# Where the sums of a fast matrix product, their casts and their low parts stand in the order of a kernel written out by hand

## The chip, the cores and the metric

The kernel runs on one core of a Trainium2 chip. The metric is the device time of one execution in microseconds (us). Engines: TensorE (PE) multiplies, VectorE (DVE), ScalarE (ACT) and GpSimd (POOL) work element by element, SyncE (SP) issues the DMAs. Each engine runs its own instructions strictly in the order in which they were emitted.

## The reference, cut to what matters

```python
# q, k, v: (2 batches, 8 heads, 768 tokens, 64) f32; lam: one decay per head
out = decay_attention(q, k, v, lam)           # in blocks, with a decaying state
x = out.transpose(0, 2, 1, 3).reshape(1536, 512)
h = x @ w_in;  x = (h * tanh(softplus(h))) @ w_out      # 512 -> 2048 -> 512, mish
h = x @ w_in2; return (h * sigmoid(h)) @ w_out2         # the same sizes, silu
```

All is f32. The weights reach the chip as 64-bit floats and are decoded there.

## The kernel before

Attention comes first: 12 chunks of 128 tokens, each giving 128 columns of x. Then two layers, mm 0 and mm 1, over three token tiles of 512 (t = 0, 1, 2). A weight block n (0 to 15 in layer 0, 16 to 31 in layer 1) has an input half (n, 0) and an output half (n, 1), of 128x512 each. `emit_h(t, n)` makes one 128x512 tile of the hidden values with 12 matmuls, `emit_o(t, n)` adds its share to four output banks with 12 more.

**Precision.** Each f32 operand is split into a high part (a cast on ACT to fp32r: xh, wh, gh, sh, th) and a low part (value minus high part: xl, wl, gl, sl, tl), and three of the four cross products are multiplied. The low parts of weights (`run_parts`, L175 and L176) and of hidden values (`activate`, L395 to L399) are made on POOL.

**Decoding.** `split_w(n, i)` queues five DVE operations (L129 to L137) in `todo`; from the middle of group 4 on the first of them runs on ACT (L93). The fifth frees one of the four load slots, and `pump` then issues the next load on SP. `run_split(k)` emits the next k operations of `todo`. A finished decode goes to `parts`; the next `run_parts` emits its cast and low part. `dec` has four buffers.

**Steps and groups.** Twelve steps (the loop at L621) interleave attention with layer 0 for the first blocks. Step 8 is the first without attention. From step 8 on the kernel also prepares a fast product for tiles 0 and 1: with x cut in quarters, seven products (`Block.m1` to `m7`, six matmuls each, L535) stand for eight. Four of their x operands are `sums[0]` to `sums[3]`, made once per layer from the quarters: f1 = a21 + a22 (sum 0), f2 = f1 - a11 (sum 1), f3 = a11 - a21 (sum 2), a12 - f2 (sum 3). The weights get four subtractions too, `sum_pair(p)` (L161), through a one-buffer tile `t4` that f3 of layer 0 and s1 of layer 1 share.

Seven groups g = 1 to 7 follow, of four weight blocks each (n0 = 4g), two blocks A and B of seven products each. A group is a list of 30 items, emitted in order (L686): the products, four fills (the outputs of tile 2 from the group before), o(0,f) and o(1,f) (outputs of tiles 0 and 1), and hs (hidden values of tile 2). After each item come the parts, `run_rest`, `run_sums` and `run_split`. In groups 1 and 4 (`g in (1, NG)`, the first of each layer) the order of the A products leaves room: A.m1, fill, A.m2, fill, fill, A.m5, A.m6, fill, A.m7, A.m3, A.m4.

Within a block A.m1 is copied by ACT to bank b (L554) before A.m2 continues in its bank; A.m5 is copied by ACT (L559); after m6 DVE adds b to that into c (L543), after m7 into e; m7 waits for the first add and m4 for the second.

**Sums before.** `make_sums` (layer 0) queues fourteen single operations in `summing`, where `xsplit` is a cast on ACT with its low part on DVE; steps 8 to 11 each emit four. `evac` of tile 1 at the end of group 3 queues seven entries for layer 1; there two of the four low parts run on POOL. Each of the next items emits two entries (`run_sums(2)`). The tiles' own casts and low parts are `part(j)` (L465, L467): the cast at once, the low part on POOL from the queue `rest`, one for each item, without regard to the tile.

Of the kernel before, what the change touches and what calls it, by code (L numbers as in the profile page):

```python
# [17 lines left out]
def decay_attention_mish_silu_kernel(  # L18
# [353 lines left out]
    def bank(name):  # L372
        nbank[0] += 1
        if late and nbank[0] % 2:
            return late[2].tile([P, T], F32, tag="x", name=name)
        return ps_h.tile([P, T], F32, tag="h", name=name)

    def run_rest(k):
        for _ in range(min(k, len(rest))):
            rest.pop(0)()  # L380

    def run_sums(k):
        for _ in range(min(k, len(summing))):
            summing.pop(0)()

    def run_later():
        while later:
# [15 lines left out]
    def emit_h(t, n, first=False):  # L403
        mm = n // NF
        xt = x_tile(t)
        assert (n, 0) in ready
# [12 lines left out]
        activate(ph, mm, t, n)  # L419
# [20 lines left out]
        if last:  # L440
            evac(mm, n % NF // GF, t)

    def xsplit(hi, lo, f, eng=None):
        nc.scalar.copy(hi, f)
        (eng or nc.gpsimd).tensor_tensor(out=lo, in0=f, in1=hi.bitcast(F32), op=ALU.subtract)

    def evac(mm, g, t):
        if g == 0:
            accs[mm, t] = (accp if t == 0 else late[1]).tile([P, 4, T], F32, tag="acc", name="acc")
        acc = accs[mm, t]  # L450
        for j in range(4):
# [12 lines left out]
        def part(j):  # L464
            nc.scalar.copy(xh[:, j, :], acc[:, j, :])  # L465
            rest.append(
                lambda: nc.gpsimd.tensor_tensor(  # L467
                    out=xl[:, j, :], in0=acc[:, j, :], in1=xh[:, j, :].bitcast(F32), op=ALU.subtract
                )
            )  # L470
# [6 lines left out]
        s1 = late[0].tile([P, 2, T], F32, tag="t4", name="s1", bufs=1)  # L477
        tt, add, sub = nc.vector.tensor_tensor, ALU.add, ALU.subtract

        s2, s3, s4 = a1[:, 0:2], a2[:, 0:2], a1[:, 2:4]  # L480
        summing.extend([
            lambda: tt(out=s1, in0=a2[:, 0:2], in1=a2[:, 2:4], op=add),
            lambda: xsplit(*sums[0], s1, nc.vector),
            lambda: (tt(out=s3, in0=a1[:, 0:2], in1=s3, op=sub), tt(out=s2, in0=s1, in1=s2, op=sub)),  # L484
            lambda: (xsplit(*sums[1], s2), tt(out=s4, in0=s4, in1=s2, op=sub)),
            lambda: xsplit(*sums[2], s3, nc.vector),
            lambda: xsplit(*sums[3], s4),
            lambda: (part(2), part(3)),
        ])

    sums = []
# [2 lines left out]
    def make_sums():  # L494

        x0, x1 = x_tile(0), x_tile(1)
        sh, sl = [late[0].tile([P, 3, 2, T], F32R, tag=t, name=t, bufs=1) for t in ("sh", "sl")]
        sums.extend((sh[:, i], sl[:, i]) for i in range(3))
        sums.append((x1[0][:, 0:2], x1[1][:, 0:2]))
        q = lambda xt, k: [xt[i][:, 2 * k : 2 * k + 2].bitcast(F32) for i in (0, 1)]  # L500
        a11, a12, a21, a22 = q(x0, 0), q(x0, 1), q(x1, 0), q(x1, 1)
        tmp = late[1].tile([P, 4, T], F32, tag="acc", name="tmp")
        f1, f2 = tmp[:, 0:2], tmp[:, 2:4]
        f3 = late[0].tile([P, 2, T], F32, tag="t4", name="s3", bufs=1)
        add, sub = ALU.add, ALU.subtract
        tt = lambda out, in0, in1, op: lambda: nc.vector.tensor_tensor(out=out, in0=in0, in1=in1, op=op)
        split = lambda i, f: lambda: xsplit(*sums[i], f, nc.vector)
        summing.extend([
            tt(f1, a21[0], a22[0], add), tt(f1, f1, a21[1], add), tt(f1, f1, a22[1], add),
            tt(f3, a11[0], a21[0], sub), split(0, f1), tt(f3, f3, a11[1], add), tt(f3, f3, a21[1], sub),  # L510
            tt(f2, f1, a11[0], sub), split(2, f3), tt(f2, f2, a11[1], sub),
            tt(f1, a12[0], f2, sub), split(1, f2), tt(f1, f1, a12[1], add), split(3, f1),
        ])

    class Block:
# [105 lines left out]
    for i, (t, f) in enumerate(steps):  # L621
        n = i + PH
        if n == N:
# [17 lines left out]
        run_parts()  # L641
        if n < N and i != LAG:
            emit_S(n, *((ps_o, "o") if i < LAG else (ps_a, "a")))
        run_split((6, 3, 4, 4, 4, 4, 4, 4, 4, 4, 4, 4)[i])
        emit_h(t, f, f == 0)
        if n < N:
            run_parts()
# [4 lines left out]
        if i >= LAG:  # L652
            t2, f2 = steps[i - LAG]
            emit_o(t2, f2, f2 == 0, f2 == GF - 1)
        run_sums(4)
        run_rest(2)
        if n < N:
            xfinish()
        run_split((2, 0, 4, 4, 4, 4, 4, 4, 4, 4, 4, 4)[i])
        pump()  # L660

    fills = [lambda s=s: emit_o(*s, False, s[1] == GF - 1) for s in steps[-LAG:]]
    for g in range(1, 2 * NG):
# [8 lines left out]
        if nxt[0]:  # L672
            nxt[0].append(lambda: sum_pair(pa + 2))
        fill = [[fn, sp(split_w, n0 + j, 1)] for j, fn in enumerate(fills + [lambda: None] * (4 - len(fills)))]
        fill[0].append(lambda: sum_pair(pa + 1))
        fill[3] += nxt[0]
        if g in (1, NG):
            items = [[A.m1], fill[0], [A.m2], fill[1], fill[2], [A.m5], [A.m6], fill[3], [A.m7], [A.m3], [A.m4]]
# [71 lines left out]
```

## Time and profile before

| | |
|---|---|
| median of 3 runs | 615.98 us (615.7 to 616.32) |
| profiled execution | 613.99 us, span 612.2 us |
| PE busy | 573.4 us, 94% |
| DVE busy | 408.0 us, 67% |
| POOL busy | 323.0 us, 53% |
| ACT busy | 242.6 us, 40% |

The span is what the trace covers, from the first instruction to the last. A row of the timeline gives start, length, engine, line, operation, out<-in, shapes and a count of equal instructions that follow each other; in brackets stands the idle time of the engine just before, and what released it. A matmul's length overlaps that of the next; start to start counts.

### The profile page before, as it was taken

The numbers are of one execution on the slowest core, as the hardware profiler recorded it, in microseconds if no ns is written. First come the engines' busy times: TensorE is split into PE (matmuls) and PEld (weight loads), VectorE is DVE, ScalarE is ACT, GpSimd is POOL, SyncE is SP. The second block draws the span as 40 slices with busy tenths as digits, with TensorE's granted clock in tenths as the row PEclk, the third lists the DMA queues.
The fourth block names the chain that finished last, engine by engine and source line by source line (L and its number), as shares of the span: only waits on it lengthen the run. The fifth ranks groups of instructions, "written<-read, shape, count | busy, mean of one in ns | idle before, by whom it ended". The sixth has DMA issues, their size and how long they took to land.

```text
span 612.2 us, 7499 instructions
## 1 busy us (share of the span) xinstructions
PE 573.4 (94%) x2858; PEld 464.3 (76%) x2858; DVE 408.0 (67%) x530; ACT 242.6 (40%) x445; POOL 323.0 (53%) x241
## 2 busy tenths in 40 slices
PE   7899999958899999999999959999999999999997
PEld 4778788846678887888786738788888888888886
DVE  3989953593997455965689799646756477647102
ACT  3444442424433242324333563544624443444320
POOL 2768774323756264445665686744565356625420
PEclk9999999998899999999999988999999999999999
DMA  7955620011233022221312113221222123200103
GB/s 260 421 182 183 247 70 0 1 37 33 68 108 100 0 68 70 70 69 35 104 35 69 36 34 96 76 70 37 92 78 70 34 70 103 70 1 1 69 1 137
DMA packets 14627, 50.55 MB, mean 83 GB/s; under 512 B 1528, under 2 KB 3072, under 8 KB 13312
## 3 DMA queue, kind: packets, MB, share of 16 engines
q1 hardware_dynamic: 14592, 50.08, 23.8%
q8 instruction: 22, 0.36, 0.2%
q14 instruction: 13, 0.11, 0.1%
HBM read 46.92 MB, written 3.15 MB: 82 GB/s over the span
## 4 chain that ended last, share of the span: by engine, by line
PE 55%; DVE 15%; ACT 2%; issue 1%; POOL 1%; DVEq 0%; ACTq 0%
PE po L437 29%; PE ph L414 10%; PE b L535 7%; PE a L535 5%; DVE dec L135 3%; DVE dec L133 2%; PE c L535 2%; PE e L535 2%; DVE dec L137 2%; DVE dec L131 2%; DVE acc L455 2%; DVE dec L129 1%; DVE t L161 1%; DVE acc L484 1%; POOL gl L399 0%
## 5 line engine op out<-in xcount | busy, mean ns | idle before, releaser
L399 POOL TENSOR_TENSOR gl<-wa,gh 128x512 fp32r<-128x512 f32 x96 | 138.3, 1447 | 119.0 <-ACT gh L398 60.0
L176 POOL TENSOR_TENSOR wl<-dec,wh 128x512 fp32r<-128x512 f32 x64 | 87.2, 1362 | 110.3 <-ACT wh L175 108.3
L455 DVE TENSOR_TENSOR acc<-po,acc 128x512 f32<-128x512 f32 x72 | 46.9, 687 | 77.7 <-PE po L437 77.7
L437 PE MATMUL po<-gh,wh 128*128 128x512 f32 x192 | 76.7, 400 | 3.5 <-ACT gh L398 1.9
L437 PE MATMUL po<-gh,wl 128*128 128x512 f32 x192 | 75.1, 391 | 2.2 <-POOL wl L176 2.2
L437 PE MATMUL po<-wh,gh 128*128 128x512 f32 x192 | 74.8, 390 | 1.3 <-ACT acc L453 1.3
L437 PE MATMUL po<-wl,gh 128*128 128x512 f32 x192 | 74.7, 389 | 0.0
L437 PE MATMUL po<-wh,gl 128*128 128x512 f32 x192 | 74.7, 389 | 0.0
L131 DVE TENSOR_SCALAR dec<-dec 128x512 f32<-128x512 f32 x64 | 48.2, 754 | 34.8 <-ACT dec L93 33.6
L175 ACT CAST wh<-dec 128x512 fp32r<-128x512 f32 x64 | 39.6, 619 | 75.3 <-DVE dec L137 75.2
L137 DVE SCALAR_TENSOR_TENSOR dec<-slot,dec 128x512 uint32<-128x512 uint32 x64 | 66.3, 1036 | 1.8
L395 ACT ACTIVATE wa<-ph 128x512 f32<-128x512 f32 x40 | 24.0, 599 | 108.5 <-PE ph L414 94.5
L135 DVE SCALAR_TENSOR_TENSOR dec<-slot,dec 128x512 uint32<-128x512 uint32 x64 | 65.6, 1025 | 1.9
L414 PE MATMUL ph<-xh,wh 128*128 128x512 f32 x160 | 63.2, 395 | 0.2 <-ACT xh L356 0.2
L414 PE MATMUL ph<-xl,wh 128*128 128x512 f32 x160 | 60.8, 389 | 0.0
L398 ACT CAST gh<-wa 128x512 fp32r<-128x512 f32 x96 | 58.3, 623 | 1.1
L133 DVE TENSOR_SCALAR dec<-dec 128x512 uint32<-128x512 uint32 x64 | 52.6, 822 | 1.9
L437 PE MATMUL po<-gl,wh 128*128 128x512 f32 x192 | 51.5, 390 | 0.0
L437 PEld LDWEIGHTS po<-gh,wh 128*128 128x128 f32 x192 | 36.2, 189 | 14.8 <-DVE acc L455 4.3
L176 POOL TENSOR_TENSOR tl<-t,th 128x512 fp32r<-128x512 f32 x28 | 37.9, 1356 | 14.4 <-ACT th L175 14.4
L414 PE MATMUL ph<-xh,wl 128*128 128x512 f32 x160 | 44.2, 389 | 0.0
L437 PEld LDWEIGHTS po<-gh,wl 128*128 128x128 f32 x192 | 36.2, 189 | 10.1 <-POOL wl L176 3.1
(107 smaller groups left out, 983.8 us busy)
## 6 DMA issues: line engine op xcount, KB each, us to landing
slot<-w SPq DMA_DIRECT2D x64, 512.0 KB, 3.7
xslot<-x SPq DMA_DIRECT2D x10, 1024.0 KB, 9.0
out<-acc SPq DMA_DIRECT2D x12, 256.0 KB, 2.1
xslot<-x SPq DMA_DIRECT2D x4, 512.0 KB, 4.3
dmask<-scr SPq DMA_DIRECT2D x2, 256.0 KB, 4.1
lamrow<-scr SPq DMA_DIRECT2D x2, 128.0 KB, 5.2
pw<-lam SPq DMA_DIRECT2D x1, 0.0 KB
scr<-pw SPq DMA_DIRECT2D x1, 8.0 KB
```

Source lines behind the costliest of these rows:

```text
L131: nc.vector.tensor_scalar(out=df, in0=df, scalar1=2.0**-15, scalar2=None, op0=ALU.max)
L133: nc.vector.tensor_scalar(out=d, in0=d, scalar1=3, scalar2=0x3FFFFFF8, op0=shl, op1=band)
L135: nc.vector.scalar_tensor_tensor(out=d, in0=low, scalar=29, in1=d, op0=shr, op1=bor)
L137: nc.vector.scalar_tensor_tensor(out=d, in0=high, scalar=0xC0000000, in1=d, op0=band, op1=bor)
L175: nc.scalar.copy(hi, f)
L176: nc.gpsimd.tensor_tensor(out=lo, in0=f, in1=hi.bitcast(F32), op=ALU.subtract)
L398: nc.scalar.copy(gh, a)
L399: nc.gpsimd.tensor_tensor(out=gl, in0=a, in1=gh.bitcast(F32), op=ALU.subtract)
L414: nc.tensor.matmul(ph, lhsT=wi[wsel][:, kk * P : (kk + 1) * P], rhs=xt[xsel][:, kk, :], start=(i == 0), stop=(i == 3 * KD - 1),)
L437: nc.tensor.matmul(po[t][j], lhsT=lhsT, rhs=rhs, start=(first and wsel + gsel == 0), stop=(last and gsel == 1))
L455: nc.vector.tensor_tensor(out=acc[:, j, :], in0=po[t][j], in1=acc[:, j, :], op=ALU.add)
L535: nc.tensor.matmul(self.b[dst], lhsT=w[ws][:, kk * P : (kk + 1) * P], rhs=x[xx][:, kk, :], start=(start and i == 0), stop=(i == 5), skip_g ...
```

## The change

`summing` now holds lists: one entry is a stage of several operations, and each step or item emits one entry. In layer 0 four entries replace fourteen; each begins with the sum's cast, then come operations of other sums, and the low part comes last. In layer 1 eight entries replace seven, and all four low parts run on DVE.

The pair of weights 6 and 7 is queued in step 11 instead of 10, and steps 9 to 11 decode nothing until two operations at the end of step 11. In group 1 decoding starts with item 0, not item 6: two operations after a product, four after a fill up to item 10; from item 20 on the extra operation goes. In group 4 the items before 9 decode nothing, but for four at item 6, which are the four subtractions of pair 9 (queued ahead of the output weights there); neither does the last item of group 3. In all groups a fill before item 11 is followed by three operations instead of two (four in group 1).

`rest` entries carry their tile and part: group 4 emits two of them at item 7 and none at items 8 to 13. Two assertions at build time say that a tile's low parts have been emitted before they are read; they emit nothing.

```diff
-            summing.pop(0)()
+            for fn in summing.pop(0):
+                fn()
...
-    def xsplit(hi, lo, f, eng=None):
-        nc.scalar.copy(hi, f)
-        (eng or nc.gpsimd).tensor_tensor(out=lo, in0=f, in1=hi.bitcast(F32), op=ALU.subtract)
+    def cast(i, f):
+        return lambda: nc.scalar.copy(sums[i][0], f)
+
+    def low(i, f):
+        hi, lo = sums[i]
+        return lambda: nc.vector.tensor_tensor(out=lo, in0=f, in1=hi.bitcast(F32), op=ALU.subtract)
...
         summing.extend([
-            lambda: tt(out=s1, in0=a2[:, 0:2], in1=a2[:, 2:4], op=add),
-            lambda: xsplit(*sums[0], s1, nc.vector),
-            lambda: (tt(out=s3, in0=a1[:, 0:2], in1=s3, op=sub), tt(out=s2, in0=s1, in1=s2, op=sub)),
-            lambda: (xsplit(*sums[1], s2), tt(out=s4, in0=s4, in1=s2, op=sub)),
-            lambda: xsplit(*sums[2], s3, nc.vector),
-            lambda: xsplit(*sums[3], s4),
-            lambda: (part(2), part(3)),
+            [tt(f1, a2[:, 0:2], a2[:, 2:4], add)],
+            [cast(0, f1)],
+            [low(0, f1), tt(f1, f1, a1[:, 0:2], sub)],
+            [cast(1, f1), tt(f4, f4, f1, sub)],
+            [low(1, f1), tt(f3, a1[:, 0:2], f3, sub), cast(3, f4)],
+            [cast(2, f3), low(3, f4)],
+            [low(2, f3)],
+            [lambda: part(2), lambda: part(3)],
         ])
...
         summing.extend([
-            tt(f1, a21[0], a22[0], add), tt(f1, f1, a21[1], add), tt(f1, f1, a22[1], add),
-            tt(f3, a11[0], a21[0], sub), split(0, f1), tt(f3, f3, a11[1], add), tt(f3, f3, a21[1], sub),
-            tt(f2, f1, a11[0], sub), split(2, f3), tt(f2, f2, a11[1], sub),
-            tt(f1, a12[0], f2, sub), split(1, f2), tt(f1, f1, a12[1], add), split(3, f1),
+            [tt(f1, a21[0], a22[0], add), tt(f1, f1, a21[1], add), tt(f1, f1, a22[1], add), tt(f2, f1, a11[0], sub)],
+            [cast(0, f1), tt(f2, f2, a11[1], sub), tt(f3, a11[0], a21[0], sub), tt(f3, f3, a11[1], add), low(0, f1)],
+            [cast(1, f2), tt(f1, a12[0], f2, sub), tt(f1, f1, a12[1], add), tt(f3, f3, a21[1], sub), low(1, f2)],
+            [cast(3, f1), cast(2, f3), low(3, f1), low(2, f3)],
         ])
...
-        if i == 10:
+        if i == len(steps) - 1:
             split_pair(3)
...
-        run_split((6, 3, 4, 4, 4, 4, 4, 4, 4, 4, 4, 4)[i])
+        run_split((6, 3, 4, 4, 4, 4, 4, 4, 4, 0, 0, 0)[i])
...
-        run_sums(4)
+        run_sums(1)
...
-        run_split((2, 0, 4, 4, 4, 4, 4, 4, 4, 4, 4, 4)[i])
+        run_split((2, 0, 4, 4, 4, 4, 4, 4, 0, 0, 0, 2)[i])
...
-        fill[0].append(lambda: sum_pair(pa + 1))
+        fill[0].insert(1 if g == NG else 2, lambda: sum_pair(pa + 1))
...
-            run_rest(1)
-            run_sums(2)
+            run_rest(2 if g == NG and at == 7 else 0 if g == NG and 8 <= at < 14 else 1)
+            run_sums(1)
             small = isinstance(getattr(item[0], "__self__", None), Block)
-            k = 1 if small else 3 if item[0] in hs else 2
-            run_split(k if g not in (1, NG) else 0 if at < 6 else k + 1)
+            k = 1 if small else 3 if item[0] in hs or at < 11 else 2
+            if g == NG and at < 9 or g == NG - 1 and at == len(items) - 1:
+                k = 4 if g == NG and at == 6 else 0
+            elif g in (1, NG) and at < 20:
+                k += 1
+            run_split(k)
```

## Rows read from the trace of the kernel before

**Rows 1.** The page's first part: busy us, share of the span, instructions.
```profile
PE 573.4 (94%) x2858; PEld 464.3 (76%) x2858; DVE 408.0 (67%) x530; ACT 242.6 (40%) x445; POOL 323.0 (53%) x241
```
**Rows 2.** Busy us of each engine in three stretches, granted clock (PEclk), DMA share.
```profile
126.63:186.09 59.46, 46.53 (x181) 35.20 (x180) 47.94 (x59) 23.68 (x42) 29.18 (x21) 0.91 0.22 71
330.33:393.70 63.37, 51.91 (x206) 40.08 (x205) 56.66 (x57) 30.88 (x53) 42.75 (x28) 0.95 0.21 67
402.00:442.00 40.00, 40.00 (x178) 33.14 (x177) 22.75 (x28) 21.67 (x40) 19.49 (x14) 1.00 0.20 67
```
**Rows 3.** The chain of waits in group 4's later part: start, us, what.
```profile
410.02 1.36 PE a L535 x6
412.74 2.72 PE po L437 x12
```
**Rows 4.** Timeline of TensorE in group 1, instructions that waited.
```profile
130.07 0.50 PE L437 MATMUL po<-gh,wh 128*128 128x512 f32 x1 [1.91 <-ACT gh L398]
139.52 1.22 PE L535 MATMUL a<-xh,wh 128*128 128x512 f32 x2 [6.29 <-ACT b L554]
...
159.76 1.20 PE L535 MATMUL a<-xh,wh 128*128 128x512 f32 x2 [2.38 <-ACT b L554]
...
182.81 0.50 PE L437 MATMUL po<-gh,wh 128*128 128x512 f32 x1 [0.75 <-DVE acc L455]
```
**Rows 5.** Timeline of ACT before the second product of group 1.
```profile
137.42 1.04 ACT L444 CAST xh<-tmp 128x1024 fp32r<-128x1024 f32 x1 [3.75 <-DVE tmp L506]
...
138.89 0.58 ACT L554 COPY b<-a 128x512 f32<-128x512 f32 x1
```
**Rows 6.** Timeline of DVE: first sums, and group 1.
```profile
119.45 3.58 DVE L506 TENSOR_TENSOR s<-s,xl 128x1024 f32<-128x1024 f32 x2
...
128.45 1.23 DVE L506 TENSOR_TENSOR tmp<-xh,tmp 128x1024 f32<-128x1024 f32 x1
...
148.21 0.70 DVE L543 TENSOR_TENSOR c<-b,m 128x512 f32<-128x512 f32 x1 [8.49 <-PE b L535]
...
149.73 0.43 DVE L133 TENSOR_SCALAR dec<-dec 128x512 uint32<-128x512 uint32 x1
...
150.92 0.69 DVE L137 SCALAR_TENSOR_TENSOR dec<-slot,dec 128x512 uint32<-128x512 uint32 x1
...
156.45 1.40 DVE L133 TENSOR_SCALAR dec<-dec 128x512 uint32<-128x512 uint32 x1
```
**Rows 7.** Timeline of POOL, beside busy DVE and beside idle DVE.
```profile
156.09 2.87 POOL L399 TENSOR_TENSOR gl<-wa,gh 128x512 fp32r<-128x512 f32 x2
...
304.63 1.26 POOL L176 TENSOR_TENSOR wl<-dec,wh 128x512 fp32r<-128x512 f32 x1
```
**Rows 8.** Timeline of TensorE in group 2, the one wait.
```profile
241.99 0.50 PE L437 MATMUL po<-gh,wl 128*128 128x512 f32 x1 [1.10 <-POOL wl L176]
```
**Rows 9.** Timeline of TensorE in group 4, instructions that waited.
```profile
332.73 0.50 PE L437 MATMUL po<-gh,wh 128*128 128x512 f32 x1 [0.88 <-DVE acc L455]
...
337.42 0.73 PE L535 MATMUL a<-xh,wh 128*128 128x512 f32 x2 [1.22 <-ACT b L554]
...
357.81 1.19 PE L535 MATMUL b<-xh,th 128*128 128x512 f32 x2 [4.24 <-ACT wh L175]
...
367.02 0.73 PE L535 MATMUL a<-xh,wh 128*128 128x512 f32 x2 [3.26 <-ACT b L554]
```
**Rows 10.** Timeline of DVE before the fourth product of group 4.
```profile
352.64 2.47 DVE L455 TENSOR_TENSOR acc<-po,acc 128x512 f32<-128x512 f32 x4
...
356.98 0.69 DVE L543 TENSOR_TENSOR e<-b,m 128x512 f32<-128x512 f32 x1
```
**Rows 11.** Timeline of POOL in group 4: low parts.
```profile
346.37 3.40 POOL L445 TENSOR_TENSOR xl<-acc,xh 128x1024 fp32r<-128x1024 f32 x1
...
359.10 1.46 POOL L467 TENSOR_TENSOR xl<-acc,xh 128x512 fp32r<-128x512 f32 x1
360.52 1.48 POOL L176 TENSOR_TENSOR tl<-t,th 128x512 fp32r<-128x512 f32 x1
```

More of the change, by code (lines that the diff above doesn't have):

```diff
@@ L379, in run_rest @@
         for _ in range(min(k, len(rest))):
-            rest.pop(0)()
+            rest.pop(0)[1]()
     def run_sums(k):
         for _ in range(min(k, len(summing))):
-            summing.pop(0)()
+            for fn in summing.pop(0):
+                fn()
     def run_later():
@@ L405, in emit_h @@
         xt = x_tile(t)
-        assert (n, 0) in ready
+        assert (n, 0) in ready and not any(key[0] == t for key, _ in rest)
         wi = wtiles[n, 0]
@@ L441, in emit_o, with tt @@
             evac(mm, n % NF // GF, t)
-    def xsplit(hi, lo, f, eng=None):
-        nc.scalar.copy(hi, f)
-        (eng or nc.gpsimd).tensor_tensor(out=lo, in0=f, in1=hi.bitcast(F32), op=ALU.subtract)
+    def cast(i, f):
[3 more added lines that the diff above has]
+        return lambda: nc.vector.tensor_tensor(out=lo, in0=f, in1=hi.bitcast(F32), op=ALU.subtract)
+    def tt(out, in0, in1, op):
+        return lambda: nc.vector.tensor_tensor(out=out, in0=in0, in1=in1, op=op)
     def evac(mm, g, t):
@@ L465, in part @@
             nc.scalar.copy(xh[:, j, :], acc[:, j, :])
-            rest.append(
+            rest.append((
+                (t, j),
                 lambda: nc.gpsimd.tensor_tensor(
                     out=xl[:, j, :], in0=acc[:, j, :], in1=xh[:, j, :].bitcast(F32), op=ALU.subtract
-                )
-            )
+                ),
+            ))
         if t != 1:
@@ L476, in evac @@
         a1, a2 = accs[0, 0], acc
-        s1 = late[0].tile([P, 2, T], F32, tag="t4", name="s1", bufs=1)
-        tt, add, sub = nc.vector.tensor_tensor, ALU.add, ALU.subtract
-        s2, s3, s4 = a1[:, 0:2], a2[:, 0:2], a1[:, 2:4]
+        f1 = late[0].tile([P, 2, T], F32, tag="t4", name="s1", bufs=1)
+        f3, f4 = a2[:, 0:2], a1[:, 2:4]
+        add, sub = ALU.add, ALU.subtract
         summing.extend([
-            lambda: tt(out=s1, in0=a2[:, 0:2], in1=a2[:, 2:4], op=add),
-            lambda: xsplit(*sums[0], s1, nc.vector),
-            lambda: (tt(out=s3, in0=a1[:, 0:2], in1=s3, op=sub), tt(out=s2, in0=s1, in1=s2, op=sub)),
-            lambda: (xsplit(*sums[1], s2), tt(out=s4, in0=s4, in1=s2, op=sub)),
-            lambda: xsplit(*sums[2], s3, nc.vector),
-            lambda: xsplit(*sums[3], s4),
-            lambda: (part(2), part(3)),
+            [tt(f1, a2[:, 0:2], a2[:, 2:4], add)],
[6 more added lines that the diff above has]
+            [lambda: part(2), lambda: part(3)],
         ])
@@ L505, in make_sums @@
         add, sub = ALU.add, ALU.subtract
-        tt = lambda out, in0, in1, op: lambda: nc.vector.tensor_tensor(out=out, in0=in0, in1=in1, op=op)
-        split = lambda i, f: lambda: xsplit(*sums[i], f, nc.vector)
         summing.extend([
-            tt(f1, a21[0], a22[0], add), tt(f1, f1, a21[1], add), tt(f1, f1, a22[1], add),
-            tt(f3, a11[0], a21[0], sub), split(0, f1), tt(f3, f3, a11[1], add), tt(f3, f3, a21[1], sub),
-            tt(f2, f1, a11[0], sub), split(2, f3), tt(f2, f2, a11[1], sub),
-            tt(f1, a12[0], f2, sub), split(1, f2), tt(f1, f1, a12[1], add), split(3, f1),
+            [tt(f1, a21[0], a22[0], add), tt(f1, f1, a21[1], add), tt(f1, f1, a22[1], add), tt(f2, f1, a11[0], sub)],
+            [cast(0, f1), tt(f2, f2, a11[1], sub), tt(f3, a11[0], a21[0], sub), tt(f3, f3, a11[1], add), low(0, f1)],
+            [cast(1, f2), tt(f1, a12[0], f2, sub), tt(f1, f1, a12[1], add), tt(f3, f3, a21[1], sub), low(1, f2)],
+            [cast(3, f1), cast(2, f3), low(3, f1), low(2, f3)],
         ])
@@ L524, in product @@
                 self.b[dst] = bank(dst)
+            assert isinstance(xq, int) or not any(key[0] == xq[0] and key[1] // 2 == xq[1] for key, _ in rest)
             x = sums[xq] if isinstance(xq, int) else [t[:, 2 * xq[1] : 2 * xq[1] + 2] for t in x_tile(xq[0])]
```

## The prediction

> **What bounds the kernel now.** I read the busy shares first: TensorE is busy 573.4 of 612.2 us, far more than any other engine [rows 1]. Next I compared busy time by stage. Between 402 and 442 us, inside a steady group, TensorE is busy for all 40 us and its granted clock is 1.00. In two stages it isn't: group 1 from its first product A.m1 to the end of o(1,1) (126.63 to 186.09) and group 4 over the same span (330.33 to 393.70), with clocks of 0.91 and 0.95 [rows 2].
>
> The chain of waits in the steady part gives the price of PE work: 1.36 us for a product of six matmuls, 2.72 us for an emit_o or emit_h of twelve [rows 3]. Group 1's stage holds 14 products and 8 twelves (two fills, four o(0,f), hs0, o(1,1)): 14 x 1.36 + 8 x 2.72 = 40.8 us, and takes 59.46, so 18.7 us are lost. Group 4's stage has two more fills: 46.2 us, and takes 63.37, so 17.1 are lost. VectorE (DVE) is busy 47.9 of 59.5 us there and 56.7 of 63.4: it sets the pace, with gaps.
>
> In the timeline the TensorE rows that carry a wait name the places. In group 1: 1.91 us for gh, 6.29 for the copy of product a into bank b before A.m2, 2.38 for the same copy before B.m2, 0.75 for the accumulation adds [rows 4]. After the 6.29 us the next six matmuls take 142.24 - 139.52 = 2.72 us, twice 1.36: the clock is at its lower level for about 3 us. The cause of the 6.29 stands in ScalarE's (ACT's) rows: the copy at 138.89 comes right after the cast at 137.42, the last of the input sums, which waited 3.75 us for DVE [rows 5]. The emission order put decoding of weights 6 and 7 between the sums on DVE, and ACT runs in order. DVE then idled 8.49 us before its add at 148.21 [rows 6]. In group 4 DVE is late instead: the add into e comes at 356.98, behind the accumulation adds of the third tile at 352.64 and a decode [rows 10], so A.m4 waits 4.24 us (the row names a weight cast; it starts when the add ends) and B.m2 3.26 [rows 9]. Groups 2 and 3 each wait 1.10 us at one place (1.37 with the pitch of the matmuls around it, by their starts), 241.99 and its twin at 305.95, waiting for the low part of the group's fourth output weight [rows 8].
>
> **The change, by part.**
>
> 1. *First sums (steps 8 to 11).* One stage of sums per step instead of four operations; the three passes f1, then f2 = f1 - a11 no longer sit behind f3's buffer. The low part of sum 0 still waits for its cast, which stands behind the accumulation copies, so the second half starts at 119.45 as now [rows 6]. From there four 128x1024 operations: alone 1.23 us each, two of them beside a POOL instruction 3.58 [rows 6]. I get 119.45 + 4 x 1.15 + 2 x 1.1 (two gl on POOL) = 126.3 for sum 1, the last two lows by 128.8, one more collision, then two decode operations from about 129.3. On ACT cast 3 (from 124.7, after the activation of hs3, which TensorE ends at 123.9) and cast 2 (to 126.8) no longer wait for DVE, gh(2,3) follows at once, and the copy of a can go when the product ends at 128.0. So the 1.91, the 6.29 and the slow stretch behind it go: 8.7 + 1.4 + restarts, and TensorE runs through A.m1, fill, A.m2, fill, A.m5, A.m6 until 126.63 + 4 x 1.36 + 2 x 2.72 = 137.5.
>
> 2. *What is late next.* A.m7 needs DVE's add into c. In the new order 20 decode operations stand ahead of it on DVE (weights 6 and 7, the fifth step's output weight 4, the four subtractions of pair 3, one more): three decodes of 2.71 us (0.45, 0.46, 0.46, 0.73 and 0.61 from start to start; 149.73 and 150.92 begin the third and the fifth operation of one), 1.5 and 0.45, together 10.1 us with POOL idle. Beside POOL the same operation goes from 0.43 to 1.40 [rows 6]: about 1 us for each POOL instruction, which itself takes 1.26 us with DVE idle and 1.44 beside it [rows 7]. Laid out by hand, five POOL instructions fall in: 129.3 + 10.1 + 5 = 144.4, add 0.7, so A.m7 goes at 145.1 (148.96 now). That is a wait of 7.6 us and again 1.4 us at the lower clock. Bounds: no collision gives 140.1, three more than I count give 148.
> Behind it I find 0.8 at A.m4 (add e behind six decode operations), 1.05 at B.m2 (copy of a, ACT behind gl on POOL for the buffer wa) and 2.55 at B.m7, because group 1 now decodes faster and its add c queues behind weights 6, 7 and 8. The accumulation adds at the end of o(0,3) find DVE idle, so the 0.75 and its restarts go. Lost in group 1: 7.6 + 1.4 + 0.8 + 1.05 + 2.55 = 13.4 instead of 18.7: **gain 5.3** (bounds 0 and 14).
>
> 3. *Fills with three decode operations instead of two (groups 2, 3, 5 to 7).* Group 2's 24 operations of the output weights end at item 16 instead of 19; TensorE has five items, about 9.5 us, until it needs the fourth. The 1.37 goes twice: **2.7**. Covered by DVE's slack (22.8 busy of 40 us [rows 2]); in groups 5 to 7 nothing waits there now, and nothing is gained. DMAs: holding weights 6 and 7 back frees two slots some 5 us later, so SP issues their successors later; they are needed from the eighth item on, at 146, and with the page's 3.7 us to landing are there by 141.
>
> 4. *Second sums (last item of group 3, items 0 to 6 of group 4).* Decoding stops, so DVE has only sums; the two lows that POOL did (3.40 us for the second, at 346.37 [rows 11]) go to DVE at 1.23 each. DVE has the accumulation adds ready at 332.3 (its backlog was two decode operations, now earlier), sum 0 at 333.6. ACT: copy of a at 332, ahead of cast 0, so the 0.88 and 1.22 waits go [rows 9]. Then cast 0, table load 1.3, act a, cast 1 to 338.2, cast 3, cast 2 at 341.8 to 342.8. The sums come to 344.1; A.m5 ends at 342.6, A.m6 at 343.9, the add into c at 344.9, the pair's four subtractions 346.3, the third tile's adds 348.8, add e 349.5. TensorE reaches A.m4 at 349.4 without a wait (357.81 now).
>
> 5. *The third tile's low parts held back.* POOL does two lows at item 7 and the other four later. But at item 7 ACT emits the four casts of the third tile first (they follow the adds, to 349.5), then th, th; POOL gets tl, tl and only then the two lows of tile 1 that A.m4's last matmuls read: 350.1 + 4 x 1.4 to 1.47 (prices [rows 11]) = 355.7. A.m4 ends at 356.1 instead of 350.7: 5.4 lost, and 1.4 at the lower clock. B.m2 then starts at 360.0 (367.02 now), the copy of a waiting for no one. Decoding resumes at item 9 from 349.5 on DVE; the 19 operations of output weights 16 to 19 took some 24 us with adds in the profile, so the fourth's low part comes at about 375.5, 0.5 to 1 late: 1.2 with trifles. Lost: 8.0 of 17.1, **gain 9.1** (bounds 2 and 15).
>
> A rule weighed against the rows of part 2: the Trainium skill (SBUF — State Buffer, "Who interferes with whom") says that DVE and GpSimd hold a shared port pair as an exclusive lock for a whole instruction, so that the other fully blocks. It is a rival below.
>
> Sum: 5.3 + 2.7 + 9.1 = 17.1. The profiled execution took 613.99 (span 612.2 and 1.8 around it), 2.0 under the median 615.98; by the profile it becomes 596.9, at the median 598.9. I say **599**.
>
> **Rivals.**
> - *Full blocking.* If every POOL instruction adds its whole 1.26 us to DVE instead of 1.0, nine collisions before A.m7 and B.m7 and ten in group 4's decoding cost 19 x 0.26 = 4.9 more: 604. For it: 1.26 is near the 0.97 by which a decode operation grew. Against: two gl in a row took 2.87 beside DVE [rows 7], 0.35 more than alone, while DVE did more than one operation, so the two do overlap. The Trainium skill's page on SBUF, strictly read, would give this; the row's 0.97 doesn't reach it.
> - *DVE less disturbed, lows earlier.* If POOL's instructions fall between DVE's, A.m7 starts near 140.5, and with POOL's two lows ahead of tl A.m4 isn't held: 4.7 + 5.4 less wait: 589. Against it stands the written order of item 7.
> - *The waits only change place.* DVE is the bound of both stages, its total work unchanged: group 1 gains 0, group 4 gains 2, groups 2 and 3 2.7: 611. For it: DVE is busy 56.7 of 63.4 us in group 4. Against: its 11.5 idle us in group 1, and subtractions and output weights that may end after the stage.
> - *Slower: the lower clock stays.* After the two new waits of 7.6 and 5.4 us come only short products with short waits between them. If the clock stays down through A.m7 to B.m6 (8 products, 1.36 more each, 10.9) and from A.m4 to B.m6 (5, 6.8), less the 2.8 counted, plus the first two o of each B (4 x 2.7), it costs 25.7: 625. From about 17 us on, that is seven products and three o in all, the kernel is slower. For it: clock 0.91 in group 1's stage. Against: after 6.29 and 2.38 us of waiting it was back in some 3 us [rows 4].
>
> **Numbers.** Forecast 599 (593 to 602): 0.48. Full blocking 604: 0.18. Undisturbed 589: 0.15. Changed place 611: 0.10, a quarter of it within 0.2%. Slower: 0.09. 0.2% (1.2 us) is about what a measurement of this kernel can tell from no change; faster 0.88, same 0.03, slower 0.09. For 8 in 10 the range takes in 589 and most of the way to 611: 588 to 609.
>
> **What would show it.** Right: the copy of a in group 1 at about 128, TensorE unbroken to A.m6, then one wait of 5 to 9 us at A.m7 for the add into c; no wait for the fourth output weight's low part in groups 2 and 3; in group 4 no wait until A.m4, whose last two matmuls wait some 5 us for POOL. Wrong: A.m2 still waiting for ACT, A.m7 after 148, a new wait in groups 5 to 7, or clocks below 0.9 in both stages.

## The result and the profile after

The changed kernel takes **609.88 us** (median of 4 runs, 608.31 to 610.4), against 615.84 for the kernel before on the same chip: ratio 0.9901, 95% interval [0.9879, 0.9923]. That is faster by 6.0 us where 17.1 were forecast; the time lies 0.9 us above the range. The profiled execution took 610.4 us with a span of 608.5.

The page's first part after the change (busy us, share of the span, instructions) answers to [rows 1]: no engine's total explains the result.

```profile
PE 574.0 (94%) x2858; PEld 468.3 (77%) x2858; DVE 418.8 (69%) x532; ACT 242.6 (40%) x445; POOL 324.8 (53%) x239
```

The first two stages of [rows 2], then a stretch from the end of group 1 through group 2 into group 3 (length; busy us of PE, PEld, DVE, ACT, POOL with the number of instructions; granted clock; DMA share; GB/s):

```profile
127.95:182.23 54.28, 43.78 (x181) 35.07 (x180) 49.75 (x64) 21.64 (x40) 30.68 (x22) 0.91 0.24 78
323.67:389.01 65.34, 54.05 (x205) 41.90 (x204) 56.00 (x58) 30.39 (x51) 34.40 (x25) 0.90 0.17 57
182.23:274.71 92.48, 92.48 (x409) 76.58 (x408) 57.32 (x84) 30.85 (x54) 45.01 (x33) 1.00 0.19 63
```

In the third stretch TensorE is busy for all of the 92.48 us, and so it is on to A.m1 of group 4: from 182.23 to 323.67 it takes 141.44 us without a gap at a granted clock of 1.00, where the kernel before took 144.24 (186.09 to 330.33). Group 1's stage fell from 59.46 to 54.28. Group 4's, where 9.1 us were to be gained, went from 63.2 to 65.3 (the same two marks in both kernels; in the kernel before the first matmul after o(1,1) starts at 393.53, not at the 393.70 of [rows 2]). A.m1 of group 1 starts 1.3 us later than in the profile before; over all profiles of this study that start lies between 126.6 and 128.6, in kernels with the old and with the new first sums, so I put it down to no part of the change.

TensorE's rows that carry a wait in group 1 (start, length, row, in brackets the idle time and what ended it), to be read against [rows 4]:

```profile
146.71 1.22 PE L543 MATMUL b<-sh,th 128*128 128x512 f32 x2 [7.72 <-DVE c L551]
147.73 1.05 PE L543 MATMUL b<-sh,tl 128*128 128x512 f32 x2
...
151.65 0.62 PE L543 MATMUL b<-xh,th 128*128 128x512 f32 x2
...
157.26 0.73 PE L543 MATMUL a<-xh,wh 128*128 128x512 f32 x2 [1.37 <-ACT b L562]
...
164.41 0.73 PE L543 MATMUL b<-sh,th 128*128 128x512 f32 x2 [1.42 <-DVE c L551]
```

One long wait is left, at A.m7 for the add into c. Behind it two products (A.m7, A.m3) take 151.65 - 146.71 = 4.94 us instead of 2.72: the pairs go every 0.85 us, not every 0.46. The granted clock from 146.71 to 151.14 is 0.50, the lower of its two levels (1.2 instead of 2.4 GHz).

The same view of group 4, against [rows 9]:

```profile
327.09 0.47 PE L438 MATMUL po<-gh,wh 128*128 128x512 f32 x1 [1.90 <-ACT wh L175]
...
347.30 0.70 PE L543 MATMUL b<-xh,th 128*128 128x512 f32 x2 [0.34 <-DVE e L551]
347.84 0.62 PE L543 MATMUL b<-xh,tl 128*128 128x512 f32 x2
352.21 0.50 PE L543 MATMUL b<-xl,th 128*128 128x512 f32 x1 [3.74 <-POOL xl L475]
353.88 0.79 PE L543 MATMUL b<-xl,th 128*128 128x512 f32 x1 [1.17 <-POOL xl L475]
354.47 1.05 PE L543 MATMUL a<-xh,wh 128*128 128x512 f32 x2
...
359.52 0.62 PE L543 MATMUL a<-xh,wh 128*128 128x512 f32 x2
...
376.02 0.50 PE L438 MATMUL po<-wh,gh 128*128 128x512 f32 x1 [1.34 <-ACT wh L175]
379.31 0.50 PE L438 MATMUL po<-wl,gh 128*128 128x512 f32 x1 [2.79 <-POOL wl L176]
```

By starts, against 1.36 and 2.72 us for a product and a twelve, the 19.1 us lost here (65.34 - 46.24) are: first fill, A.m2 and their slow matmuls 4.1; A.m4 6.3; the slow products behind it (354.47 to 359.52, 5.05 for 2.72) 2.3; the rest, 6.4, at o(0,3) and behind it. Only the second and third of these were in the forecast at more than 1.2. Of the 4.1, some 1.5 are the lower clock behind the wait (0.68 over the fill), and that differs from run to run: after the same wait of 1.89 us the fill took 3.20 us in e3 and 3.21 in e7 at a clock of 1.00, here 331.52 - 327.09 = 4.43.

### The profile page after: what moved, and what is told of

Read it like the earlier page. It is cut to its first block, busy times and chain, and to the rows that moved or that the text cites. A ratio compares the mean times of both kernels' runs of the same rounds, so it can differ in the third digit from the quotient of the medians.

```text
span 608.5 us, 7512 instructions
## 1 busy us (share of the span) xinstructions
PE 574.0 (94%) x2858; PEld 468.3 (77%) x2858; DVE 418.8 (69%) x532; ACT 242.6 (40%) x445; POOL 324.8 (53%) x239
## 4 chain that ended last, share of the span: by engine, by line
PE 71%; DVE 18%; ACT 4%; issue 3%; POOL 2%; DMA 1%; SPq 0%; POOLq 0%; ACTq 0%
PE po L438 35%; PE ph L415 14%; PE b L543 7%; PE a L543 5%; DVE dec L135 3%; PE c L543 2%; PE e L543 2%; DVE dec L133 2%; DVE dec L131 2%; PE px L347 2%; DVE dec L129 2%; DVE dec L137 1%; DVE t L161 1%; PE px L341 1%; DVE acc L462 1%
## 5 line engine op out<-in xcount | busy, mean ns | idle before, releaser
L400 POOL TENSOR_TENSOR gl<-wa,gh 128x512 fp32r<-128x512 f32 x96 | 140.3, 1468 | 120.3 <-PE b L543 41.8
L176 POOL TENSOR_TENSOR wl<-dec,wh 128x512 fp32r<-128x512 f32 x64 | 88.8, 1387 | 97.3 <-ACT wh L175 97.3
L137 DVE SCALAR_TENSOR_TENSOR dec<-slot,dec 128x512 uint32<-128x512 uint32 x64 | 69.3, 1083 | 1.9
L135 DVE SCALAR_TENSOR_TENSOR dec<-slot,dec 128x512 uint32<-128x512 uint32 x64 | 58.7, 917 | 2.1
L176 POOL TENSOR_TENSOR tl<-t,th 128x512 fp32r<-128x512 f32 x28 | 40.5, 1462 | 25.0 <-ACT th L175 21.5
L133 DVE TENSOR_SCALAR dec<-dec 128x512 uint32<-128x512 uint32 x64 | 49.8, 778 | 2.1
L438 PEld LDWEIGHTS po<-wl,gh 128*128 128x128 f32 x192 | 36.4, 190 | 10.8 <-POOL wl L176 3.1
```

The lines of the kernel that those rows point to most:

```text
L133: nc.vector.tensor_scalar(out=d, in0=d, scalar1=3, scalar2=0x3FFFFFF8, op0=shl, op1=band)
L135: nc.vector.scalar_tensor_tensor(out=d, in0=low, scalar=29, in1=d, op0=shr, op1=bor)
L137: nc.vector.scalar_tensor_tensor(out=d, in0=high, scalar=0xC0000000, in1=d, op0=band, op1=bor)
L176: nc.gpsimd.tensor_tensor(out=lo, in0=f, in1=hi.bitcast(F32), op=ALU.subtract)
L400: nc.gpsimd.tensor_tensor(out=gl, in0=a, in1=gh.bitcast(F32), op=ALU.subtract)
L438: nc.tensor.matmul(po[t][j], lhsT=lhsT, rhs=rhs, start=(first and wsel + gsel == 0), stop=(last and gsel == 1))
```

## The experiments

All edits are against the changed kernel; what isn't shown is as there. The stage lengths run from the first matmul of A.m1 to the first after o(1,1), each from one profile. Group 4's is good to some 1.5 us only: the changed kernel and e7 have the same order there and show 65.34 and 63.80, by the clock at the first fill.

| kernel | median us | ratio to before [95%] | group 1 | group 4 |
|---|---|---|---|---|
| before | 615.84 | | 59.46 | 63.20 |
| after | 609.88 | 0.9901 [0.9879, 0.9923] | 54.28 | 65.34 |
| e1_layer0_only | 606.36 | 0.9855 [0.9839, 0.9870] | 54.29 | 61.91 |
| e2_layer1_only | 616.31 | 1.0020 [1.0003, 1.0036] | 59.76 | 63.93 |
| e3_two_lows_first | 607.21 | 0.9866 [0.9853, 0.9879] | 54.27 | 62.15 |
| e4_third_tile_later | 610.68 | 0.9925 [0.9911, 0.9939] | 54.25 | 67.24 |
| e5_tail_held | 606.66 | 0.9859 [0.9839, 0.9879] | 54.24 | 61.66 |
| e6_no_first_tile_lows | 605.98, one run | | 54.24 | 61.16 |
| e7_group1_order | 601.70 | 0.9774 [0.9754, 0.9795] | 47.23 | 63.80 |
| e8_group1_and_old_layer1 | 599.92 | 0.9745 [0.9729, 0.9761] | 47.19 | 61.84 |
| e9_best_try | 595.12 | 0.9669 [0.9651, 0.9687] | 48.79 | 56.66 |
| e10_three_moves | 597.65 | 0.9721 [0.9704, 0.9737] | 47.20 | 60.54 |
| e11_third_tile_earlier | 606.47 | 0.9849 [0.9831, 0.9868] | 54.28 | 62.38 |
| e12_first_step_on_act | 595.50 | 0.9673 [0.9658, 0.9688] | 47.20 | 57.31 |

**The two halves apart.** First the new order of layer 0 and of the fills alone, layer 1 summed and decoded as before:

```diff
-            [cast(0, f1)],
-            [low(0, f1), tt(f1, f1, a1[:, 0:2], sub)],
...
+            [cast(0, f1), low(0, f1)],
+            [tt(f3, a1[:, 0:2], f3, sub), tt(s2, f1, s2, sub)],
+            [cast(1, s2), plow(1, s2), tt(f4, f4, s2, sub)],    # plow: the low part on POOL
...
-            run_rest(2 if g == NG and at == 7 else 0 if g == NG and 8 <= at < 14 else 1)
-            run_sums(1)
+            run_rest(1)
+            run_sums(2)
...
+            if g == NG:
+                k = 0 if at < 6 else k + 1
```

> Layer 0's part of the change alone: stages of sums in steps 8 to 11, early decoding in group 1, three operations after a fill; layer 1's sums, lows and decoding in group 4 as before. Theory S (the two parts add up, and group 4's part is a loss of 2.1 us, as its stage grew from 63.4 to 65.5): 607 to 608.5, that is faster than the whole change, with group 4's stage at 62 to 64 us. Rival I (the parts need each other: group 4 is late because group 3 now decodes otherwise, whatever its own order): group 4's stage stays at 65 or more, and the time at 610 or above.

It is faster than the whole change: 0.9855. The other half alone:

```diff
-            [tt(f1, a21[0], a22[0], add), tt(f1, f1, a21[1], add), tt(f1, f1, a22[1], add), tt(f2, f1, a11[0], sub)],
...
+            [tt(f1, a21[0], a22[0], add)], [tt(f1, f1, a21[1], add)], [tt(f1, f1, a22[1], add)],
...
-        run_sums(1)
+        run_sums(4)
...
+            elif g == 1:
+                k = 0 if at < 6 else k + 1
```

> Layer 1's part alone (its sums all on DVE, lows held back, decoding held back in group 4, no decoding at the last item of group 3); steps 8 to 11 and group 1, 2 and 3 as before. Theory S: no gain, 616 to 619, with waits for POOL's lows at A.m4 and for the fourth output weight at o(0,3). Rival I: with group 3 as before the accumulation adds of the second tile start in time, and the part gains 2 to 4 us: 612 to 614.

It brings no gain: 1.0020, interval [1.0003, 1.0036], if anything a little slower. So the gains of the forecast's first and third parts are there, and those of layer 1's part, more than half of the sum, went missing. The halves' 8.8 us and -1.1 come to 7.7, the whole is 6.0; the intervals of the three ratios, taken together, are as wide as the difference, so no interaction is shown.

The wait at group 4's first fill goes with the other half, though. It is there in e1, with layer 1's old order:

```profile
325.99 0.47 PE L438 MATMUL po<-gh,wh 128*128 128x512 f32 x1 [1.89 <-ACT wh L175]
```

In e2, with the new order, it is 0.86, as in the kernel before (0.88 [rows 9]). So what makes it longer is the decoding in the groups before.

**A.m4: two lows ahead of tl.** Tile 1's two lows are emitted at item 6, so POOL makes them before tl:

```diff
-            run_rest(2 if g == NG and at == 7 else 0 if g == NG and 8 <= at < 14 else 1)
+            run_rest(0 if g == NG and 7 <= at < 14 else 1)
+            if g == NG and at == 6:
+                run_rest(2)
```

> The whole change, but the two low parts of tile 1 that A.m4 reads are emitted at item 6 of group 4, ahead of the pair's two on POOL, which is idle there for 9 us. Theory W (each wait is worth its length): the waits of 3.74 and 1.17 us at A.m4 and the low clock behind them go, 6 to 7.5 us: 602.5 to 604. Rival V (DVE sets the stage's end: TensorE comes earlier to B.m7 and o(0,3) and waits there for DVE): A.m4 is free but the wait at o(0,3) grows to 6 to 9 us, and only the 3.2 us come back that DVE idled before its add in block B: 606 to 607.5.

607.21. TensorE in this run:

```profile
347.11 0.70 PE L543 MATMUL b<-xh,th 128*128 128x512 f32 x2 [1.90 <-DVE e L551]
...
353.85 0.74 PE L543 MATMUL a<-xh,wh 128*128 128x512 f32 x2 [2.38 <-ACT b L562]
...
371.51 0.50 PE L438 MATMUL po<-wh,gh 128*128 128x512 f32 x1 [1.42 <-ACT wh L175]
374.80 0.79 PE L438 MATMUL po<-wl,gh 128*128 128x512 f32 x1 [2.79 <-POOL wl L176]
```

The waits for POOL at A.m4 are gone, as part 5 had them in the order tl, tl, xl, xl; but the add e and the copy at B.m2, which they had covered, are late in their place, and the two waits at o(0,3) stay as they were. Of the 6.3 us at A.m4 and the 2.3 behind it the stage keeps 3.2, and 1.5 of these stand at the first fill, ahead of the edit, where this profile's clock did not fall; against e7's stage of 63.80 the edit itself brings 1.65.

**o(0,3): the third tile's lows later, and earlier.**

```diff
-            run_rest(2 if g == NG and at == 7 else 0 if g == NG and 8 <= at < 14 else 1)
+            run_rest(2 if g == NG and at == 7 else 0 if g == NG and 8 <= at < 18 else 1)    # e4; e11: < 11
```

> The whole change, but the other four low parts of the third tile go out at items 18 to 21 of group 4 instead of 14 to 17. Theory P (at o(0,3) the fourth output weight's low part stands on POOL behind two of them and two gl): the wait of 2.79 us there goes and most of the low clock after it, 4 to 5 us: 605 to 606. Rival D (that weight's decoding on DVE is what comes late): the cast's 1.34 stays, the low part follows 1.9 us later, and the gain is 1 us or less: 609.

> The whole change, but the third tile's other four low parts go out at items 11 to 14 of group 4 instead of 14 to 17. If their place on POOL ahead of the fourth output weight is what made o(0,3) late: the wait of 2.79 us there falls to about 1.1, the low clock behind it mostly goes, 606.5 to 608. If DVE's decoding is late by itself: the cast's wait stays at 1.3 and the low part's at 2 or more, 609 to 610.

Later doesn't help: 610.68, with the stage 1.9 us longer. The wait of o(0,3) for the low part falls to 0.61, and hs0, which reads the third tile's low parts, takes it over:

```profile
374.63 0.50 PE L438 MATMUL po<-wl,gh 128*128 128x512 f32 x1 [0.61 <-POOL wl L176]
...
382.52 0.79 PE L415 MATMUL ph<-xl,wh 128*128 128x512 f32 x1 [3.76 <-POOL xl L475]
```

Earlier does: 606.47, the stage 3.0 us shorter. The waits in that run:

```profile
375.69 0.50 PE L438 MATMUL po<-wh,gh 128*128 128x512 f32 x1 [1.47 <-ACT wh L175]
377.04 0.50 PE L438 MATMUL po<-wl,gh 128*128 128x512 f32 x1 [0.85 <-POOL wl L176]
```

So the longer wait at o(0,3) is mostly POOL's order (2.79 to 0.85). The wait for the cast (1.34, and 1.47 here) is DVE's decode, which ends as the cast starts (375.32 and 375.35 in the changed kernel); but POOL's instructions lengthen it. In e4, where the four lows come behind the decode, it takes 26.1 us (346.43 to 372.56) instead of 28.3 (347.06 to 375.32), and the wait for the cast is gone; in e11 the four still fall beside it, and it takes 28.8.

**The first fill.** Here part 4 saw no wait. The last three decode operations of group 3, which stand ahead of the second tile's adds, go to item 0 of group 4:

```diff
-                k = 4 if g == NG and at == 6 else 0
+                k = 4 if g == NG and at == 6 else 3 if g == NG and at == 0 else 0
+            elif g == NG - 1 and at > 26:
+                k = 0
```

> The whole change, but the last three decode operations of group 3 (weight 19) are held back from before the accumulation adds of the second tile to item 0 of group 4, between the first sum and its low part. Theory V (in group 4 DVE's total sets the end): the wait of 1.9 us at the fill and its low clock go, but the sums come no earlier, new waits of 1 to 2 us stand at A.m7 or A.m4, and the gain is 0 to 2 us: 608 to 610. Rival W (each wait is worth its length): 4 us, 606.

606.66, the stage 3.7 us shorter: the fill's wait and the slow matmuls behind it are gone, and a later one (A.m4's add e, 1.53 instead of 0.34) gives 1.2 back. In the changed kernel the wait at 327.09 carries the name of a weight's cast on ACT (326.38). In this run that cast comes only at 328.57, and the fill starts at 324.61 without a wait, so the cast was not what it waited for. What ended the wait were these adds on DVE, here of the changed kernel and then of the run with the tail held:

```profile
326.26 2.48 DVE L462 TENSOR_TENSOR acc<-po,acc 128x512 f32<-128x512 f32 x4
```

```profile
322.94 2.47 DVE L462 TENSOR_TENSOR acc<-po,acc 128x512 f32<-128x512 f32 x4
```

**What the decode operations there cost.** The low parts of tile 0 in layer 1, four instructions on POOL, are left out:

```diff
+            if t == 0:
+                return
```

> The whole change, but the four low parts of the first tile at the end of group 3 (128x512 on POOL, between 306 and 317 us) are left out: the low parts of the layer before stay in their place. Theory C (POOL's instructions lengthen DVE's beside them, about 1 us each): the 18 DVE operations between the accumulation adds of the first and the second tile take 18 to 19 us instead of 22.4, and the adds of the second tile start with TensorE's end, without the wait of 1.9 us. Rival N (DVE is late for its own count of operations or for a load): 21 us or more, and the wait stays.

The stretch runs from the first decode operation behind the first tile's accumulation adds to the second tile's adds, in the kernel before, the changed one and this run. In this run it is taken to the end of the last decode operation, since the adds then wait 2.10 us for TensorE. (Columns as in [rows 2]; the last of the (x) is the count of POOL's instructions, with one that only touches an end.)

```profile
310.49:332.00 21.51, 21.36 (x95) 17.36 (x93) 21.03 (x21) 8.45 (x15) 16.52 (x13) 1.00 0.19 63
```

```profile
303.84:326.26 22.42, 21.36 (x95) 17.35 (x93) 21.98 (x19) 8.28 (x15) 19.44 (x13) 1.00 0.15 47
```

```profile
303.65:320.91 17.26, 17.26 (x78) 14.30 (x77) 16.81 (x19) 6.88 (x13) 12.23 (x8) 1.00 0.18 61
```

The two last hold the same 18 decode operations and subtractions on DVE, some 9.2 us without POOL at the prediction's prices (two decodes of 2.71, 2.25 and 1.5). With 13 instructions of POOL beside them they take 22.42, with 8 (the four left out, and one that now falls behind) 17.26: 5.16 us for five, **1.03 us each**; and (22.42 - 9.2) / 13 gives 1.02. The rows show it one by one: in the changed kernel 13 of DVE's 18 operations are longer by 1.0 to 1.1 us, in this run 8. One of the subtractions, there and here:

```profile
309.94 1.52 DVE L161 TENSOR_TENSOR t<-dec 128x256 f32<-128x256 f32 x1
```

```profile
309.73 0.41 DVE L161 TENSOR_TENSOR t<-dec 128x256 f32<-128x256 f32 x1
```

So the price in the prediction's second part, 1.0, was right, and full blocking at 1.26 was not. The count was wrong: the kernel before has 20 operations in this stretch, the changed one 18, but POOL is busy for 19.44 us of it instead of 16.52, about two more instructions, and 13 of DVE's operations are lengthened instead of 11. Two operations less (-0.9) and two collisions more (+2.0) make the adds 1 us later, not earlier. In e1 the stretch is the same to 0.01 us (302.74 to 325.15): the count comes from the decoding of the groups before, not from layer 1's order.

**Group 1's wait at A.m7.** Pair 3's subtractions are queued ahead of the first output weight, and decoding is dealt so that less of it stands ahead of the adds into c and e:

```diff
-        fill[0].insert(1 if g == NG else 2, lambda: sum_pair(pa + 1))
+        fill[0].insert(1 if g in (1, NG) else 2, lambda: sum_pair(pa + 1))
+            if g == 1 and at < 20:
+                k = (2, 2, 2, 2, 0, 0, 4, 0, 2, 1, 2, 2, 1, 2, 2, 3, 2, 2, 3, 2)[at]
```

> The whole change, but in group 1 eight decode operations instead of eighteen stand between the sums and the add into c, the pair's subtractions come right after that add, and the output weights follow (two at most at an item up to the fifth product of block B). Theory A (the 7.7 us wait at A.m7 is only a matter of what stands ahead of that add; DVE's total fits into the stage): the wait falls to about 1, the low clock behind it goes, group 1's stage falls from 54.3 to 44 to 47 us, 600 to 603. Rival B (DVE's total sets the stage's end, as in group 4): the waits come back at B.m7 and at the output weights, the stage stays above 50: 606 or more.

601.70. The wait of 7.72 us becomes 1.30, and the clock stays at 1.00:

```profile
140.58 0.73 PE L543 MATMUL b<-sh,th 128*128 128x512 f32 x2 [1.30 <-DVE c L551]
```

```profile
128.24:175.47 47.23, 42.41 (x182) 33.40 (x181) 44.72 (x55) 20.55 (x38) 26.27 (x19) 1.00 0.23 78
```

The 7.1 us that the stage gains are more than the 6.4 of the wait: with it goes the slow stretch behind, and two waits of 0.8 come new inside one of the output twelves. That DVE's queue is what A.m7 waited for is shown by this.

**Together.** This order of group 1 with layer 1 as in e1:

> The order of e7 in group 1 together with layer 1's sums, lows and decoding of the kernel before (as in e1, 606.4). If the stages add: e1's time less e7's gain over the whole change. Theory A: 597 to 599.5; rival B: 603 or more.

599.92, both stages as in the runs with one edit each. Then the moves of e7, e3 and e5 in one kernel:

> e7's order in group 1, e3's two low parts at item 6 of group 4 and e5's three held operations together. If the moves add: e7 601.7, less 3.2 (e3's stage) and 3.7 (e5's): group 4's stage at 57 to 58, 594.5 to 596. If DVE's total is the bound of group 4 by now, the second move gives back part: stage 60 or more, 598 or more; the waits then stand at e's add before A.m4 and at o(0,3).

597.65, group 4's stage 60.54. Less 3.2 and 3.7, 65.34 would give 58.4, but both differences hold the same 1.5 us of lower clock at the first fill. From e7's 63.80, which is free of it, the two moves are worth 1.65 and 2.14, which gives 60.0: that they add only in part isn't shown. TensorE's waits in that stage:

```profile
337.77 0.70 PE L543 MATMUL b<-xh,th 128*128 128x512 f32 x2 [2.99 <-DVE e L551]
...
362.17 0.50 PE L438 MATMUL po<-wh,gh 128*128 128x512 f32 x1 [1.43 <-ACT wh L175]
365.47 0.79 PE L438 MATMUL po<-wl,gh 128*128 128x512 f32 x1 [2.79 <-POOL wl L176]
```

What is left is DVE (the add e) and o(0,3). The next version also lets ACT take the first operation of two more decodes and emits the third tile's lows from item 11:

```diff
-            if g == NG and at == 7:
+            if g == NG and at == 3:
                 silu.append(True)
...
-            run_rest(2 if g == NG and at == 7 else 0 if g == NG and 8 <= at < 14 else 1)
+            run_rest(0 if g == NG and 7 <= at < 11 else 1)    # with the moves of e7, e3, e5
```

> As e10, and in group 4 the output weights 17 and 18 have their first decode step on ACT too (two DVE operations fewer), and the third tile's four low parts go out at items 11 to 14, where POOL was idle between 358 and 361 us. If DVE and POOL's order before o(0,3) is what bounds the stage: the waits of 1.3 and 2.8 us at o(0,3) shrink to 2 or less together, 3 to 5 us under e10: 590 to 593. If the low parts only displace others on POOL: within 1 us of e10.

595.12, the fastest here: 0.9669 [0.9651, 0.9687]. To tell its two new edits apart, the first of them alone on top of e10:

> e10 (597.65) with the first decode step of output weights 17 and 18 on ACT, and nothing else. If DVE's count is the bound of group 4: two operations of 1.4 us less, 595 to 596. If POOL's order is: within 0.7 us of e10, and e9's gain of 2.5 us came from the place of the low parts.

595.50, the same within the intervals. The second edit adds nothing that the medians can tell, though alone, in e11, it was worth some 3 us: the waits that it shortened there are gone here without it. (Group 1, with the same order as in e10, ran in e9's profile at a granted clock of 0.97 rather than 1.00: 48.79 us; that stage is not part of this comparison.) The stage goes from 60.54 to 57.31 by two operations fewer on DVE (its instructions fall from 532 to 530), and the two waits at o(0,3) give way to one of 0.74. The wait for the copy at B.m2 falls from 2.37 to 0.78, and that for the add e at B.m4 grows from 0.67 to 2.04:

```profile
339.50 1.04 PE L543 MATMUL b<-xh,th 128*128 128x512 f32 x2 [3.00 <-DVE e L551]
...
359.47 0.74 PE L543 MATMUL b<-xh,th 128*128 128x512 f32 x2 [2.04 <-DVE e L551]
...
366.66 0.50 PE L438 MATMUL po<-wh,gl 128*128 128x512 f32 x1 [0.74 <-POOL gl L400]
```

## Why the prediction was wrong

**Parts 1 and 2, right.** The copy of a goes 1.6 us after A.m1 starts, TensorE runs unbroken to the end of A.m6, and group 1 gains 5.2 where 5.3 stood. Inside it A.m7's wait was 7.7 (7.6 forecast); the slow products behind it lost 2.2, not 1.4; A.m4 waits for nothing (0.8 forecast), B.m2 and B.m7 lose some 1.7 each (1.05 and 2.55). That the sum fits to 0.1 us is luck: behind A.m7's wait each term misses by 0.6 to 0.9, and they cancel. DVE's rows ahead of A.m7, 20 decode operations from 130.88:

```profile
144.57 1.48 DVE L129 TENSOR_SCALAR dec<-slot 128x512 uint32<-128x512 uint32 x1
145.97 0.69 DVE L551 TENSOR_TENSOR c<-b,m 128x512 f32<-128x512 f32 x1
```

15.1 us for them, the forecast's 10.1 plus 5 collisions; five of the 20 are lengthened.

**Part 3, right.** Groups 2 and 3 gain 1.4 us each, 2.8 in all against 2.7. In group 5, where nothing was to change, TensorE waits once for ACT (0.45 us at B.m2), and 0.8 us are lost from there on: ACT has three first decode steps ahead of that copy (426.71, 1.82 us) and had two before. The prediction had named such a wait as a sign of being wrong. And the stretch that makes the adds of part 4 late comes with this half of the change, as e1 shows.

**Part 4, wrong at "DVE has the accumulation adds ready at 332.3 (its backlog was two decode operations, now earlier)".** That is 2.0 us after A.m1 starts; they ended 5.1 us after (328.74). I took two operations off DVE's backlog and did not lay POOL's instructions beside the 18 that stay, though the price of each, 1.0 us, stood two paragraphs above. They decide: 13 of them against 9.2 us of DVE's own work. The first fill then waits 1.90 us and the clock drops: 4.1 us, with 0 forecast, of which 1.5 are a clock that stayed up in other runs after the same wait. e5 and e6 show the cause from both sides.

**Part 5, right at A.m4, wrong at o(0,3).** A.m4 lost 6.3 (5.4 forecast), by the order tl, tl, xl, xl that was read from the code, as e3 shows. The clock behind it cost 2.3 rather than 1.4. "0.5 to 1 late: 1.2 with trifles" for o(0,3) was 6.4: 4.1 of waits, the rest at the lower clock behind them. I had put the fourth weight's low part 26.0 us behind the first operation of DVE's train of output weights (349.5 to 375.5) and TensorE 0.5 to 1 us ahead of it. In the changed kernel they come 32.2 (379.27 - 347.06) and 27.6 us behind it. DVE's rows there:

```profile
347.06 0.42 DVE L129 TENSOR_SCALAR dec<-slot 128x512 uint32<-128x512 uint32 x1
...
362.52 0.70 DVE L551 TENSOR_TENSOR c<-b,m 128x512 f32<-128x512 f32 x1 [3.16 <-ACT gh L399]
...
373.65 1.67 DVE L137 SCALAR_TENSOR_TENSOR dec<-slot,dec 128x512 uint32<-128x512 uint32 x1
```

For 3.16 us DVE stands at the add into c of B with decode operations queued behind it, because A.m4's wait made B.m6 late (by its starts it ends at 362.2; the cast that the row names ran just then, 361.91 to 362.53, but in e11 the same wait, 2.22 us, is for B.m6). That isn't the whole cause: in e3 DVE doesn't stand, the train takes the forecast's 24 us, TensorE is there earlier as well, and the waits are the same. What stays in both runs is POOL's order. The lows that were held back come out here, all four of the third tile inside this train, and the fourth weight's low part stands behind two of them and two gl:

```profile
365.36 2.92 POOL L475 TENSOR_TENSOR xl<-acc,xh 128x512 fp32r<-128x512 f32 x2
...
371.60 3.17 POOL L475 TENSOR_TENSOR xl<-acc,xh 128x512 fp32r<-128x512 f32 x2
374.73 3.13 POOL L400 TENSOR_TENSOR gl<-wa,gh 128x512 fp32r<-128x512 f32 x2
377.82 1.45 POOL L176 TENSOR_TENSOR wl<-dec,wh 128x512 fp32r<-128x512 f32 x1
```

e11, in which all four are done 6 us earlier (368.6 instead of 374.8), takes 1.9 us of the 2.79 away, and e4 shows the other side: with the lows behind the train both waits nearly go, and hs0 waits for them instead.

Group 4's miss, by its terms: first fill 4.1, A.m4 0.9, its clock 0.9, o(0,3) 5.2, together 11.1. The profiled run took 13.5 us more than the 596.9 forecast for it: these 11.1, group 5's 0.8, and 1.3 by which A.m1 of group 1 started later, 13.2 in all. Between the medians (598.9 and 609.88) it is 11.0.

**The rivals.** Full blocking is out by size (1.03 us, above). So is a DVE less disturbed, with A.m7 near 140.5: five POOL instructions lengthened five of the operations ahead of it, and at item 7 the lows came behind tl as written. That the waits only change place, with DVE as the bound of both stages, was forecast at 611, near the time measured, but not for its reason: group 1 did gain 5.2, and group 4 lost. Of group 4 alone it is near the truth: e3, e4 and e5 each moved a part of their wait on, and the last 3.2 us came from two operations taken off DVE. That the lower clock stays is out: it was back after two products both times.

## What to carry to other kernels

Price each run of operations on VectorE together with the GpSimd instructions that will fall beside it, again for every stretch that an edit shifts: the unit price may be right and the count still decide. Work that is held back has to be followed to the place where it comes out, and the queue there has to be laid out anew; a duration from the profile before holds only for the neighbours that it had there. When a stage's waits follow each other on one engine, removing one gives part of its length and the next wait takes the rest; work taken off that engine shortens the stage (two operations less in e12: 3.2 us), even where one of the waits grows. And before two moves' gains are added up, see whether both hold the same piece, as here the lower clock at the first fill.

## What the runs showed of the hardware

A GpSimd instruction costs VectorE 1.0 us whether it comes alone (the fourth subtraction of a pair in group 1 took 1.49 rather than 0.42) or in an unbroken train (1.03, by e6), less than the 1.26 us that it takes with VectorE idle [rows 7]. The Trainium skill (SBUF — State Buffer, "Who interferes with whom") has the two engines, where they contend, exclude each other for whole instructions; these rows bear that out in kind and not in size.

What a wait costs in clock can't be told from its length. After 7.72 us at A.m7 and after 3.74 and 1.17 at A.m4 the next two products went at a granted clock of 0.50, 2.2 and 2.3 us lost. After 1.90 us at the first fill of group 4 its 12 matmuls took 4.43 us instead of 2.72 (0.68), and after 1.89 at the same place 3.20 in e3 and 3.21 in e7, at 1.00. After 3.26 us at B.m2 of group 4 the kernel before lost 1.6 us and e1 nothing. What decides it, no run here shows.

A wait's named releaser can be a bystander. The row at 327.09 names a cast on ACT; in e5 that cast comes 2.2 us later, DVE's adds 3.3 us earlier, and the wait is gone.
